# Eight slots of a threshold attention: block transposes and DMA exchanged for TensorE turns with an identity

## The chip, the cores and the metric

The kernel runs on one core of a Trainium2 chip. The metric is the device time of one execution in microseconds, as the median over runs. TensorE (PE) multiplies, with its weight loads shown as PEld; VectorE (DVE), ScalarE (ACT) and GpSimd (POOL) work on vectors; SyncE (SP) issues most DMA transfers. [...]

## The reference

Attention with a threshold, for 8 batches, 8 heads, 576 positions and 64 numbers a head, and then a dense block on the 4608 tokens of 512 numbers:

```
scores = (q @ k^T) / 8
thresh = max(scores) - tau                   # per row
scores = where(scores >= thresh, scores, -1e9)
attn   = exp(scores - max(scores));  attn = attn / (sum(attn) + 1e-9)
x      = attn @ v                            # tokens of 8 heads x 64 = 512
h      = x @ w_in                            # 512 -> 1024
solu   = h * softmax(h)
ln     = (solu - mean) / sqrt(var + 1e-6) * g_ln
out    = ln @ w_out                          # 1024 -> 512
```

All is float32 but the two weight matrices, which arrive as 8-byte floats and are taken apart by integer operations (16 pieces of 512 KB).

## The kernel before

**Slots and rounds.** A slot is one attention step: for a pair of heads (`hp`, four pairs a batch), 128 query rows for each of the two heads, against all 576 keys. There are 144 slots, 18 a batch; two slots (`r` 0 and 1) make a unit, whose product with v is done in one go. The first eight slots are the four units of batch 0, `kind` 0. The program is written out by hand, round by round, under a manual schedule; round `rnd` holds the steps of slot `rnd` and later steps of earlier slots.

**A slot's steps.** `scores` (L480): eight products of 64x64 tiles of the array into two PSUM tiles of 128x576, one a head. `maxes` (L502): VectorE finds the negated row maximum plus tau (`nth`) for each. `ramp` (L517): ScalarE turns scores into distances to the threshold; what lies under the threshold becomes hugely negative. `exps` (L526): the exponential, with the row sum. In the next round `normalise` (L533 to L536): GpSimd adds 1e-9, takes the power -1 and scales both tiles by it. Then `blocks` (L548): VectorE transposes 32x32 blocks of each tile into `T`; after the second slot of a unit three DMAs (L557, L559) move the blocks between partitions into `wT`. Some rounds later (`LAG_PV`, `pv_due`) `attend_steps` (L590) makes the unit's 36 products with v, and `attended` (L622) copies the result into `xh`, one part of the tokens.

**The dense block.** When the four pairs of a group of tokens are there, the group is `ready`: two parts of 128 tokens, each with four steps, at most one a round: two of `ff_h` (L655) and two of `ff_o` (L760), with vector steps between. `ff_o` needs all of w_out (`w2_done`, true from the end of round 16).

**What stands around it in the first rounds.** `whole_pair` (L434) turns q and k of pair 1, 2, 3 of the batch by products with an identity (L345), in rounds 0, 2 and 4; it needs both spare PSUM tiles. These two tiles, p0 and p1, are handed out by `take` from the list `pairs_free`; the products with v and the dense block use them too. The two tiles of `scores` are apart from them and single. One weight piece a round is decoded (L286 to L309 on VectorE, L291 on ScalarE, L319 on GpSimd), until round 15; its raw data are loaded four rounds ahead by SP. `w` has four buffers, `wT` two, `T` two.

Of the kernel before, what the change touches and what calls it, by code (L numbers as in the profile page):

```python
# [8 lines left out]
F32 = mybir.dt.float32  # L9
# [4 lines left out]
ALU = mybir.AluOpType  # L14
# [6 lines left out]
def kernel(  # L21
# [49 lines left out]
    w1 = const.tile([P, NP, DFF], F32, name="w1")  # L71
    w2 = const.tile([P, 2 * NC, DM], F32, name="w2")
    w1_parts = w1.rearrange("p c (a g x) -> p c g a x", g=2, x=32)
    mhalf = const.tile([P, 1], F32, name="mhalf")
    mone = const.tile([P, 2], F32, name="mone")
    mark = const.tile([P, 1], F32, name="mark")
# [143 lines left out]
    def constants():  # L220

        nc.gpsimd.memset(lims[0], 0.0)
        nc.scalar.activation(out=ntau, in_=lims[0], func=AF.Exp)
        make_identity(nc, ident)
        for g in range(2):
            of = 64 + 32 * (1 - g)
            nc.gpsimd.tensor_copy(
                out=swapped[ROWS[1], 32 * g : 32 * g + 32], in_=ident[ROWS[1], of : of + 32]
            )
        nc.gpsimd.memset(mhalf, -0.5)  # L230
        nc.gpsimd.memset(mone, -1.0)
# [282 lines left out]

    def ramp(s, x):
        d = live[s]
        nc.scalar.activation(  # L517
            out=d["w"][x], in_=d["w"][x] if d["loose"] else d["ps"][x][:, 0:S], func=AF.Prelu, bias=d["nth"][x], scale=-1.0,
            alpha=1.0e30,
        )  # L520

    def exps(s):
        d = live[s]
        d["sm"] = sm = small.tile([P, 2], F32, tag="sm", name="sm")
        for x, w in enumerate(d["w"]):
# [279 lines left out]
    pv_due = []  # L805
    for s, (b, kind, hp, r) in enumerate(slots):
        if r == 1:
            pv_due.append((s + LAG_PV + (s < 6 or s in (11, PER - 1, PER + 9)), (b, kind, hp)))

    def first_slot(i):  # L810
        return PER * (i // NP) + 2 * (i % NP)
# [56 lines left out]
    with tc.manual_schedule():  # L868
# [13 lines left out]


        pieces = {r: x for x, r in enumerate(range(16))}
        whole = {0: 1, 2: 2, 4: 3}
        for r, hf, parts in ((0, 0, (0,)), (1, 0, (1, 2)), (3, 1, (0,)), (5, 1, (1, 2))):
            load_at[r] = [lambda hf=hf, parts=parts: load_v(0, hf, parts)]

# [9 lines left out]
        while True:  # L898
# [10 lines left out]
            if rnd == NS:  # L909
# [6 lines left out]
                    cur = None  # L916
                    quarter = 0
                assert quarter != 3
            if rnd == 13:
                prev, cur, quarter = cur, None, 0  # L920
            if (
                cur is None and quarter == 0 and ready and ready[0][0] <= rnd
# [9 lines left out]
            if more:  # L932
                room = SPARE
                if busy and quarter > 1 and preps and rnd + 4 < first_slot(preps[0][3]):
                    room = 0
                while preps and preps[0][0] <= rnd and preps[0][1] <= room:
                    _, n, make, _ = preps.pop(0)
                    items.append(make())
                    room -= n
                scores(rnd, items)  # L940
                if rnd == 0:
                    turned(dict(first, base=576, eased=True), [q_item(0, slice(1, 4))])
                    pairs_free += tags
                idle = quarter == 0 and cur is None and (
                    prev is None or bool(pv_due) and pv_due[0][0] <= rnd
                )
                loose = idle and rnd > NW
                if loose:
                    keeps(rnd, 0)
                    keeps(rnd, 1)  # L950
                maxes(rnd, loose)
                ramp(rnd, 0)
                if rnd == 0:
                    weight_a(0)
                if not loose:
                    keeps(rnd, 0)
                    keeps(rnd, 1)
                ramp(rnd, 1)
                exps(rnd)
            if rnd in whole:  # L960
                whole_pair(whole[rnd])
            if rnd - 1 in live:
                normalise(rnd - 1)
            if rnd - 1 in pieces:
                weight_c(pieces[rnd - 1])
# [22 lines left out]
            if step == ("h", 0):  # L988
                ff_h(cur, 0, rnd + 1 < NS, beside)
                quarter = 1  # L990
            elif step == ("h", 1):
                ff_h(cur, 1, None, beside)
                quarter = 2
                by = rnd + 2 * (rnd == 14)
                late.setdefault(by, []).append(lambda t=cur: (ff_max(t), ff_exp(t)))
                late.setdefault(by + 1, []).append(lambda t=cur: (ff_mul(t), ff_sum(t)))
                middle.setdefault(by + 2, []).append(lambda t=cur: ff_stats(t))
                if rnd + 6 < NS:
                    norms[by + 3] = cur
                else:  # L1000
                    late.setdefault(rnd + 2, []).append(lambda t=cur: ff_norm(t))
                middle.setdefault(by + 3, []).append(lambda t=cur: (ff_norm2(t), ff_swap(t)))

                at = by + 4 if more or not ready or len(ready[0][1][0]) == 1 else rnd + 6
                if cur == (0, 1, 1):
                    middle.setdefault(rnd + 6, []).append(lambda t=cur, at=rnd + 6: ff_turn(t, at))
                else:
                    late.setdefault(at, []).append(lambda t=cur, at=at: ff_turn(t, at))
                if not more:
                    between.append(cur)  # L1010
                    cur = None
                    quarter = 0
            elif step == ("o", 0):
                if prev is not None:
                    ff_o(prev, 0)
                quarter = 3
            elif step == ("o", 1):
                if prev is not None:
                    ff_o(prev, 1)
                    last = not (more or ready or cur or between)  # L1020
                    begin.setdefault(rnd + 1, []).append(lambda t=prev, last=last: ff_out(t, last))
                    late.setdefault(rnd + 1, []).append(lambda t=prev, last=last: ff_store(t, last))
                prev, cur = cur, None
                quarter = 0
            if attending is not None:
# [5 lines left out]
                    ready.append((rnd + 1, [(b // 2,)]))  # L1031
                elif kind < 2 and hp == NP - 1:
                    ready.append((rnd + 1, [(b, kind, 0), (b, kind, 1)]))
            if rnd - 1 in live:
                blocks(rnd - 1)
            for job in late.pop(rnd, []):
                job()
# [55 lines left out]
```

## Time and profile before

| what | value |
|---|---|
| median of 3 runs | 865.01 us (863.66 to 867.64) |
| profiled execution, span from first to last instruction | 867.2 us |
| profiled execution, own time | not listed apart from its span |
| TensorE busy | 822.9 us (95%) |
| VectorE busy | 681.7 us (79%) |
| ScalarE busy | 573.6 us (66%) |
| GpSimd busy | 500.2 us (58%) |
| mean granted TensorE clock | 0.976 |
| DMA | 168.54 MB, mean 194 GB/s |

The span lies inside the range of the three runs, 2.2 us above their median. In the profile, a line such as L502 is a line of the kernel before; `x280` counts instructions; a product in float32 appears as two MATMUL records. Digits of the 40 slices are tenths, 21.7 us a slice. The granted clock is the share of its full clock that TensorE was given.

### The profile page before, as it was taken

The numbers are of one execution on the slowest core, as the hardware profiler recorded it, in microseconds if no ns is written. First come the engines' busy times: TensorE is split into PE (matmuls) and PEld (weight loads), VectorE is DVE, ScalarE is ACT, GpSimd is POOL, SyncE is SP. The second block draws the span as 40 slices with busy tenths as digits, with TensorE's granted clock in tenths as the row PEclk, the third lists the DMA queues.
The fourth block names the chain that finished last, engine by engine and source line by source line (L and its number), as shares of the span: only waits on it lengthen the run. The fifth ranks groups of instructions, "written<-read, shape, count | busy, mean of one in ns | idle before, by whom it ended". The sixth has DMA issues, their size and how long they took to land.

```text
span 867.2 us, 36122 instructions
## 1 busy us (share of the span) xinstructions
PE 822.9 (95%) x15361; PEld 605.8 (70%) x15361; DVE 681.7 (79%) x1248; ACT 573.6 (66%) x1153; POOL 500.2 (58%) x938
## 2 busy tenths in 40 slices
PE   5668799989999999999999999999999999999997
PEld 3446466667677776899777766777777777777655
DVE  4988878878788888888888887888788887787361
ACT  5877876667677767777666766777677776776121
POOL 2886656556756666565656665565666655555120
PEclk9769999999999999999999999999999999999999
DMA  8999887998888878898888787888788787655312
GB/s 256 252 251 227 191 210 181 210 236 210 215 206 226 208 183 214 208 221 203 196 207 225 207 187 185 217 220 207 183 230 229 197 192 180 163 136 139 69 38 62
DMA packets 83712, 168.54 MB, mean 194 GB/s; under 512 B 15448, under 2 KB 45152, under 8 KB 83552
## 3 DMA queue, kind: packets, MB, share of 16 engines
q1 hardware_dynamic: 82416, 164.25, 76.3%
q8 instruction: 120, 1.97, 1.0%
q10 hardware_dynamic: 1136, 2.00, 0.7%
q14 instruction: 40, 0.33, 0.1%
HBM read 46.14 MB, written 9.44 MB: 64 GB/s over the span
## 4 chain that ended last, share of the span: by engine, by line
PE 79%; DMA 8%; DVE 4%; ACT 4%; SPq 2%; issue 2%; POOL 1%; ACTq 0%; DVEq 0%
PE o_ps L760 26%; PE h_ps L655 20%; PE pv L590 14%; PE s_ps L480 14%; DMA wT<-T 6%; PE h_ps L645 3%; ACT w L517 1%; DVE w L502 1%; ACT w L526 1%; DVE T L548 1%; DMA q<-in_q_dram 1%; DMA qT<-flip 1%; SPq L564 1%; DMA k<-in_k_dram 1%; SPq L559 0%
## 5 line engine op out<-in xcount | busy, mean ns | idle before, releaser
L760 PE MATMUL o_ps<-w,uT 64*64 64x256 f32 x4608 | 271.6, 378 | 1.2 <-ACT xe L622 0.6
L502 DVE CUSTOM_DVE_ANT_0 w<-s_ps,tau_t 128x576 f32<-128x576 f32 x280 | 200.0, 751 | 90.0 <-PE s_ps L480 61.6
L517 ACT ACTIVATE w<-s_ps,nth 128x576 f32<-128x576 f32 x280 | 196.9, 739 | 107.0 <-DVE nth L502 89.6
L760 PEld LDWEIGHTS o_ps<-w,uT 64*64 64x64 f32 x4608 | 212.7, 134 | 66.1 <-ACT xh L622 12.1
L536 POOL TENSOR_SCALAR w<-w,sm 128x576 f32<-128x576 f32 x288 | 222.1, 783 | 14.3
L548 DVE STREAM_TRANSPOSE T<-w 128x576 f32<-128x576 f32 x288 | 207.6, 755 | 20.6 <-POOL w L536 19.1
L655 PE MATMUL h_ps<-w,xh 64*64 64x512 f32 x1856 | 221.0, 589 | 0.1
L526 ACT ACTIVATE w<-w,ntau 128x576 f32<-128x576 f32 x288 | 219.7, 767 | 0.0
L590 PEld LDWEIGHTS pv<-wT,v 64*64 64x64 f32 x5760 | 175.2, 138 | 45.4 <-issue 24.5
L480 PE MATMUL s_ps<-kT,qT 64*64 64x64 f32 (+1 forms) x2048 | 177.1, 422 | 13.3 <-ACT w L517 10.9
L590 PE MATMUL pv<-wT,v 64*64 64x128 f32 (+1 forms) x5760 | 178.0, 266 | 10.9 <-DMA wT<-T 7.8
L655 PEld LDWEIGHTS h_ps<-w,xh 64*64 64x64 f32 x1856 | 118.0, 133 | 78.8 <-issue 45.7
L533 POOL TENSOR_SCALAR sm<-sm 128x2 f32<-128x2 f32 x144 | 37.0, 257 | 201.8 <-ACT w L526 198.5
L534 POOL TENSOR_TENSOR sm<-sm,mone 128x2 f32<-128x2 f32 x144 | 108.7, 755 | 12.0
L480 PEld LDWEIGHTS s_ps<-kT,qT 64*64 64x64 f32 x2048 | 73.0, 139 | 21.7 <-ACT w L517 15.7
L622 ACT COPY xh<-pv 128x256 f32<-128x256 f32 x64 | 25.1, 393 | 82.4 <-PE pv L590 82.4
L721 ACT ACTIVATE V<-u,nb,rs 128x1024 f32<-128x1024 f32 x36 | 44.7, 1241 | 39.3 <-POOL nb L711 32.4
L747 DVE STREAM_TRANSPOSE uT<-V 128x1024 f32<-128x1024 f32 x36 | 44.2, 1227 | 18.1 <-DMA V<-u 17.7
L526 ACT ACTIVATION_READ_ACCUMULATOR w<-w,ntau 128x1 f32 x288 | 55.6, 193 | 0.0
L685 DVE TENSOR_TENSOR u<-h_ps,u 128x1024 f32<-128x1024 f32 x36 | 42.8, 1190 | 9.8 <-ACT u L679 9.8
L726 DVE TENSOR_SCALAR u<-u,rs,nb 128x1024 f32<-128x1024 f32 x36 | 35.3, 982 | 17.6 <-ACT V L721 17.6
L670 DVE TENSOR_REDUCE hm<-h_ps 128x1 f32<-128x1024 f32 x36 | 42.9, 1192 | 4.8 <-PE h_ps L645 2.7
(90 smaller groups left out, 568.1 us busy)
## 6 DMA issues: line engine op xcount, KB each, us to landing
wT<-T SPq DMA_DIRECT2D x160, 288.0 KB, 6.7
wT<-T SPq DMA_DIRECT2D x64, 576.0 KB, 5.4
V<-u SPq DMA_DIRECT2D x144, 64.0 KB, 3.3
out_dram<-ob SPq DMA_DIRECT2D x71, 128.0 KB, 2.5
q<-in_q_dram SPq DMA_DIRECT2D x24, 288.0 KB, 5.7
qT<-flip SPq DMA_DIRECT2D x48, 144.0 KB, 4.2
k<-in_k_dram SPq DMA_DIRECT2D x24, 288.0 KB, 6.1
kT<-flip SPq DMA_DIRECT2D x48, 144.0 KB, 3.9
```

The lines of the kernel that those rows point to most:

```text
L480: nc.tensor.matmul(out=ps[h][ROWS[y], ks], lhsT=lhsT, rhs=d["kT"][ROWS[h], ks], start=True, stop=True,)
L502: nc.vector.tensor_tensor_reduce(out=w, in0=ps[:, 0:S], in1=(zero if loose else tau_t).to_broadcast([P, S]), scale=1.0, scalar=BIG, op0=AL ...
L517: nc.scalar.activation(out=d["w"][x], in_=d["w"][x] if d["loose"] else d["ps"][x][:, 0:S], func=AF.Prelu, bias=d["nth"][x], scale=-1.0, al ...
L526: nc.scalar.activation(out=w, in_=w, func=AF.Exp, bias=ntau, scale=1.0, accum_out=sm[:, x : x + 1])
L534: nc.gpsimd.tensor_tensor(out=sm, in0=sm, in1=mone, op=ALU.pow)
L536: nc.gpsimd.tensor_scalar(out=w, in0=w, scalar1=sm[:, x : x + 1], scalar2=1.0, op0=ALU.mult, op1=ALU.mult)
L548: nc.vector.transpose(out=T[:, :, r, h, :], in_=w)
L590: nc.tensor.matmul(out=to, lhsT=d["v"][ROWS[u], (h0 + h - u) % 4 if b > 1 else h0 + h, m ^ 4 * u if m < 8 and b < 2 else m,], rhs=rhs, sta ...
L655: mm = nc.tensor.matmul(out=h[ROWS[y], f], lhsT=x[ROWS[r], c, ROWS[y]], rhs=w1_parts[ROWS[r], c, part ^ r], start=part == 0 and c == 0, st ...
L721: nc.scalar.activation(out=V, in_=u, func=AF.Identity, bias=nb, scale=rs)
L747: nc.vector.transpose(out=uT, in_=d["V"].rearrange("p y (m x) -> p m y x", x=32))
L760: nc.tensor.matmul(out=d["o"][ROWS[z], 512 * (r ^ other) : 512 * (r ^ other) + 256], lhsT=d["uT"][ROWS[r], m].rearrange("p y x -> p (y x)" ...
```

## The change

For the first eight slots (`FRONT = 8`) the path from the distances to the tokens is another one:

- `ramp` writes the distances with their columns in another order, and GpSimd (`clamp`) raises what lies under -10000 to -10000.
- In the next round, `flip` turns each tile by 18 products of 64x64 with an identity into a spare PSUM tile, and `flipped` takes the exponential on the way from PSUM into `wT`. The exponential in place, the normalisation by GpSimd, the block transposes and the block transfers of these slots are left out.
- `front_product` makes a unit's 36 products with v, and 36 more with a tile of ones, which give the row sums. `front_norm` has VectorE add 1e-9, take the reciprocal and multiply, which writes the tokens to `xh` in place of the copy.
- The products of the first three units stand in two consecutive rounds each (3 and 4, 5 and 6, 7 and 8; between the two turns), those of the fourth in round 9. Before, the units' products stood in rounds 5, 7, 9 and 10.
- Pairs 2 and 3 are turned in rounds 1 and 2 instead of 2 and 4.
- The first tokens are ready a round earlier: the first four steps of the dense block stand in rounds 10 to 13 instead of 11 to 14.

```diff
+    ones = const.tile([P, 64], F32, name="ones")
...
+        nc.gpsimd.memset(ones, 1.0)
...
     def ramp(s, x):
         d = live[s]
+        to, of = d["w"][x], d["w"][x] if d["loose"] else d["ps"][x][:, 0:S]
+        if s < FRONT:
+            to = to.rearrange("p (m x c) -> p c m x", c=2, m=NK)
+            of = of.rearrange("p (c m x) -> p c m x", c=2, m=NK)
         nc.scalar.activation(
-            out=d["w"][x], in_=d["w"][x] if d["loose"] else d["ps"][x][:, 0:S], func=AF.Prelu, bias=d["nth"][x], scale=-1.0,
-            alpha=1.0e30,
-        )
+            out=to, in_=of, func=AF.Prelu, bias=d["nth"][x], scale=-1.0, alpha=1.0e30
+        )
+
+    FRONT = 8
+
+    def clamp(s, x):
+        w = live[s]["w"][x]
+        nc.gpsimd.tensor_scalar(
+            out=w, in0=w, scalar1=-1.0e4, scalar2=1.0, op0=ALU.max, op1=ALU.mult
+        )
+
+    def flip(s, h):
+        b, kind, hp, r = slots[s]
+        key = (b, kind, hp)
+        if r == 0 and h == 0:
+            wT = work.tile([P, 2, NK, 2, 2, 32], F32, tag="wT", bufs=2, name="wT")
...
+        w = live[s]["w"][h].rearrange("p (m x) -> p m x", m=NK)
+        tag, t = take("flip")
+        for m in range(NK):
+            for y in range(2):
+                nc.tensor.matmul(
+                    out=t[ROWS[y], 64 * m : 64 * m + 64], lhsT=w[ROWS[y], m],
+                    rhs=swapped[ROWS[1]] if y else ident[ROWS[0], ROWS[0]],
+                    start=True, stop=True,
+                )
+        return tag, t
+
+    def flipped(s, h, tag, t):
+        b, kind, hp, r = slots[s]
+        nc.scalar.activation(
+            out=units[b, kind, hp]["wT"][:, :, h, r],
+            in_=t[:, 0:S].rearrange("p (m x) -> p m x", x=64),
+            func=AF.Exp, bias=ntau, scale=1.0,
+        )
+        pairs_free.append(tag)
+        if h:
+            live.pop(s)
+
+    def front_product(key, ones_too):
...
+        if not ones_too:
+            tag, y = take("pv")
...
+        for m in range(NK):
+            for u in range(2):
+                for h in range(2):
+                    of = P * ones_too
+                    nc.tensor.matmul(
+                        out=y[ROWS[h], u, of : of + P],
+                        lhsT=ones[ROWS[u]] if ones_too
+                        else d["v"][ROWS[u], h0 + h, m ^ 4 * u if m < 8 else m],
+                        rhs=wT[ROWS[u], m, h].rearrange("p r x -> p (r x)"),
+                        start=m == 0, stop=m == NK - 1,
+                    )
+
+    def front_norm(key):
...
+        rec = work.tile([P, 2, P], F32, tag="T", name="rec")
+        nc.vector.tensor_scalar(
+            out=rec, in0=y[:, :, P : 2 * P], scalar1=1e-9, scalar2=None, op0=ALU.add
+        )
+        nc.vector.reciprocal(out=rec, in_=rec)
+        nc.vector.tensor_tensor(
...
+            in0=y[:, :, 0:P].rearrange("p u (r y) -> p u r y", r=2),
+            in1=rec.rearrange("p u (r y) -> p u r y", r=2), op=ALU.mult,
+        )
+        pairs_free.append(tag)
...
         if r == 1:
-            pv_due.append((s + LAG_PV + (s < 6 or s in (11, PER - 1, PER + 9)), (b, kind, hp)))
+            if s >= FRONT:
+                pv_due.append((s + LAG_PV + (s in (11, PER - 1, PER + 9)), (b, kind, hp)))
...
-        whole = {0: 1, 2: 2, 4: 3}
+        whole = {0: 1, 1: 2, 2: 3}
...
-            if rnd == 13:
+            if rnd == 12:
                 prev, cur, quarter = cur, None, 0
...
                 scores(rnd, items)
+                turned_w = [flip(rnd - 1, 0)] if 0 < rnd <= FRONT else []
+                unit = (rnd - 3) // 2
+                if 0 <= unit < FRONT // 2 and unit % 4 != 3:
+                    front_product(slots[2 * unit][0:3], rnd % 2 == 0)
...
                 maxes(rnd, loose)
                 ramp(rnd, 0)
+                if rnd < FRONT:
+                    clamp(rnd, 0)
+                if turned_w:
+                    flipped(rnd - 1, 0, *turned_w.pop())
+                    turned_w = [flip(rnd - 1, 1)]
...
                 ramp(rnd, 1)
-                exps(rnd)
+                if rnd < FRONT:
+                    clamp(rnd, 1)
+                else:
+                    exps(rnd)
+                if turned_w:
+                    flipped(rnd - 1, 1, *turned_w.pop())
+                if 0 <= unit < FRONT // 2:
+                    if unit % 4 == 3 and rnd % 2:
+                        front_product(slots[2 * unit][0:3], 0)
+                        front_product(slots[2 * unit][0:3], 1)
+                    if (rnd % 2 == 0) == (unit % 4 != 3):
+                        key = slots[2 * unit][0:3]
+                        front_norm(key)
+                        if key[2] == NP - 1:
+                            ready.append((rnd + 1, [(*key[0:2], 0), (*key[0:2], 1)]))
             if rnd in whole:
                 whole_pair(whole[rnd])
-            if rnd - 1 in live:
+            if rnd - 1 in live and rnd > FRONT:
                 normalise(rnd - 1)
...
-                by = rnd + 2 * (rnd == 14)
+                by = rnd + 2 * (rnd == 13)
...
-            if rnd - 1 in live:
+            if rnd - 1 in live and rnd > FRONT:
                 blocks(rnd - 1)
```

More of the change, by code (lines that the diff above doesn't have):

```diff
@@ new lines @@
+    FRONT = 8
[9 more added lines that the diff above has]
+            wT = work.tile([P, 2, NK, 2, 2, 32], F32, tag="wT", bufs=2, name="wT")
+            units[key] = dict(
+                wT=wT.rearrange("p a m b c x -> p (a m b c x)").rearrange(
+                    "p (m h r x) -> p m h r x", m=NK, h=2, r=2
+                )
[10 more added lines that the diff above has]
+        return tag, t
@@ new lines, in flipped @@
+    def flipped(s, h, tag, t):
[9 more added lines that the diff above has]
+    def front_product(key, ones_too):
+        b, kind, hp = key
+        unit = units[key]
+        wT = unit["wT"]
+        if not ones_too:
+            tag, y = take("pv")
+            unit["y"] = tag, y.rearrange("p (u n) -> p u n", u=2)
+        y = unit["y"][1]
+        d, h0 = source(b * NP + hp)
+        for m in range(NK):
[9 more added lines that the diff above has]
+                    )
@@ new lines, in front_norm @@
+    def front_norm(key):
+        b, kind, hp = key
+        tag, y = units.pop(key)["y"]
+        if hp == 0:
+            xh[b, kind] = work.tile(
+                [P, NP, 256], F32, tag=f"xh{(2 * b + kind) % 4}", bufs=1, name="xh"
+            )
+        rec = work.tile([P, 2, P], F32, tag="T", name="rec")
+        nc.vector.tensor_scalar(
+            out=rec, in0=y[:, :, P : 2 * P], scalar1=1e-9, scalar2=None, op0=ALU.add
+        )
+        nc.vector.reciprocal(out=rec, in_=rec)
+        nc.vector.tensor_tensor(
+            out=xh[b, kind][:, hp].rearrange("p (r u y) -> p u r y", u=2, r=2),
+            in0=y[:, :, 0:P].rearrange("p u (r y) -> p u r y", r=2),
+            in1=rec.rearrange("p u (r y) -> p u r y", r=2), op=ALU.mult,
+        )
+        pairs_free.append(tag)
```

## The prediction

> **What bounds the kernel now.** I read first the busy times in 40 slices and the table of windows, for where each engine is short; then the chain of waits of the first 200 us, for what ends last there; then the timelines of DVE, PE and POOL round by round. The page:
>
> ```profile
> span 867.2 us, 36122 instructions
> PE 822.9 (95%) x15361; PEld 605.8 (70%) x15361; DVE 681.7 (79%) x1248; ACT 573.6 (66%) x1153; POOL 500.2 (58%) x938
> PE   5668799989999999999999999999999999999997
> PEclk9769999999999999999999999999999999999999
> ```
>
> TensorE is busy 95% of the span, and its idle time lies in the first slices; there its clock is reduced too. By windows (us; busy PE, PEld, DVE, ACT, POOL; then granted clock, DMA share, GB/s):
>
> ```profile
> 20.00:40.00 20.00, 13.84 (x262) 10.13 (x258) 19.53 (x42) 17.82 (x41) 16.91 (x20) 0.67 0.89 237
> 40.00:60.00 20.00, 12.16 (x172) 6.51 (x170) 18.54 (x40) 15.75 (x32) 16.90 (x20) 0.76 1.05 251
> 60.00:80.00 20.00, 17.21 (x241) 12.75 (x240) 14.45 (x31) 12.54 (x25) 12.26 (x16) 0.81 0.95 228
> 200.00:400.00 200.00, 199.77 (x3847) 154.62 (x3843) 168.18 (x306) 140.04 (x278) 123.61 (x240) 1.00 0.84 210
> ```
>
> From 20 to 60 us VectorE is the bound (98% and 93%), TensorE two thirds busy at about 0.7 of its clock. From 200 us on TensorE has no gap, so what the front loses or gains arrives whole at the end. The chain (start, length, what) shows the one long wait of the front:
>
> ```profile
> 53.84 0.74 DVE T L548
> 54.63 0.58 SPq L557
> 55.26 0.60 SPq L559
> 55.92 12.04 DMA wT<-T
> 68.00 3.53 PE pv L590 x65
> ```
>
> The block transfer of the fourth unit (slots 6, 7) takes 12.04 us, and its product waits for it. So the scores of the rounds, from the PE timeline, start at 14.1 (round 1), 18.5, 22.9, 28.4, 33.1, 40.4, 43.2, 48.6, 53.4 (round 9), 62.6, 71.3, 75.7, and 105.6 in round 17. Rounds 1 to 8 follow VectorE: two maxima 1.36 (0.68 from start to start), two transposes 1.36, the weight piece 1.0 + 0.6 + 0.34 + 0.34, together about 5.0 us. Rounds 9 and 10 follow the transfers, 9 us each. VectorE is then the bound again (its maximum of round 11 starts at 72.5, of round 17 at 108.5), and after that TensorE.
>
> By the two instruction streams, the order on TensorE is the same from round 17 to the end. So I forecast when round 17 is reached, and add the difference.
>
> **Part by part.** *Removed* in slots 0 to 7: 16 transposes (16 x 0.68 = 11 us of VectorE, on the path in rounds 1 to 8); 12 block transfers of 4 units with their SP issues (four times 576 KB, on the path in rounds 9 and 10); POOL's add and power (8 x (0.26 + 0.76) us, beside other work); ScalarE's 16 sum reads (about 0.09 us each from start to start) and 4 copies of 0.37, beside. POOL's 16 clamps of 128x576 replace 16 scalings of that form (0.78 each). The ramp's interleaved write I price as before (0.74): the copy into kT that also pairs columns, 0.384 for 128x256, costs no more than the plain xh copy, 0.393.
>
> *Added on TensorE:* per slot two turns of 18 products of 64x64, and per unit 36 products with ones. The identity products of the trace (L345) start every 0.11 us per group of four tiles of the array at full clock (93.24, 93.30, 93.36: two products each 0.055) and every 0.22 at half. A turn uses two tiles instead of four, so 9 x 0.11 = 1.0 us at full clock if the two overlap, 1.9 if not; at half clock double. I take 1.0: tiles ran side by side in every L345 group. The ones cost what a product with v of 72 records does, 1.92 at full clock (3.90 at 36.73, at half).
>
> A round 3 to 8 on TensorE is then scores 0.97 + turns 2.0 + product 1.92 = 4.9 us at full clock, 5.0 with gaps: no less than VectorE's 5.0 before. VectorE has 3.65 left, ScalarE 2 x 0.63 + 2 x 0.67 + 0.62 = 3.2, POOL 2 x 0.74 + 1.28 = 2.8. TensorE becomes the bound of these rounds, and the 11 us taken off VectorE bring nothing by themselves.
>
> *The clock.* In 2 us windows of before the clock steps between 0.5 and 1.0 at about 23.4, 26.8, 33.6, 37.0, 40.4, 43.9, 47.3, 54.1: multiples of 3.4 us, up after a stretch filled by work, down after one with more than about 1 us of idleness (47.3 to 50.7, with 2.7 busy, kept it; 40.5 to 43.9, with 2, lost it). So a filled TensorE runs at 1.0, and each longer stall costs up to 1.7 us more by a half-clock stretch. [...] The trace shows identity products filling 20.2 to 22.4, and the clock rises at 23.4, so they count as work; at half clock a round of 4.9 would take 9.8. [...]
>
> *Rounds 1 and 2.* The pairs' turns (rounds 2 and 4 before) move to rounds 1 and 2, and take both spare PSUM tiles, which each turn of distances now occupies until its exponential. Round 1: scores end at 16.4, the turns of slot 0 at 18.4; the second exponential stands on ScalarE behind the second ramp (its maximum ends at 17.7; two ramps and two exponentials alternate at 0.65 from 17.1), so 19.7; pair turn 1.1; scores of round 2 at 20.9 instead of 18.5. The same chain again (copies of the pair 1.5, maximum, ramp, exponential): round 3 at 26.4 instead of 22.9. TensorE idles some 1.3 us in each, so I add one half-clock stretch, 1.7: 28.1.
>
> *Added on VectorE:* three operations of 128x256 per unit, waiting for the product with ones, with the next weight piece and maximum queued behind. The first and third cost 0.43 and 0.45 by the copy row (L407, 0.425). The reciprocal has no row. Low end: the copy, 0.43. High end: the only division-like rows are POOL's powers, 572 ns for 128x1 and 755 for 128x2 against 234 and 257 for an add; one more element costs 183 against 23, eight times. VectorE's copies of 64 and 256 (0.215, 0.425) give 1.1 ns an element, so 256 x 8 x 1.1 = 2.25 us + 0.15 = 2.4. I take 2.0, since a power is nearer to a division than a copy is. [...]
>
> What waits: from the end of the ones (rounds 4 and 6), VectorE needs 2.9 for the three, 2.3 for weights, 0.75 for the maximum; ScalarE 0.7 + 0.7 for ramp and exponential; only then is the tile free for the second turn: 7.35 us. TensorE has 1.0 + 0.97 + 1.0 + 1.92 = 4.9 to do meanwhile. Stall 2.45 us in rounds 5 and 7, or 0.9 at the copy's price. The longer stall also costs half-clock stretches, 2.5 us for both (of at most 3.4).
>
> *Sum.* Round 9 starts at 28.1 + 6 x 5.0 + 2 x 2.45 + 2.5 = 65.5, against 53.4. Round 9: scores and both products 4.9, the three operations 2.9, transposes and weights 3.6: VectorE's maximum of round 10 at 76.9, of round 11 (another 1.4 + 1.4 + 2.3) at 82.0, against 72.5. From there to the maximum of round 17 VectorE needed 36.0, of which some 3 us idle; the same work, with the first dense tile a round earlier, I take at 35.0. Round 17's maximum: 117.0 against 108.5, +8.5. Gained are the 12 us transfer and its neighbour; paid are 3.5 + 1.7 in rounds 1 and 2, 7.4 in 5 and 7, and the wait for the last norm. Profiled span 867.2 + 8.5 = 875.7; it lies 2.2 above the median of the runs, so 873.5, rounded to 873.
>
> **Rivals.** *Cheap reciprocal* (0.43): round 9 at 28.1 + 30 + 1.8 = 59.9, round 10's maximum at 69.7, round 17's at 109.8: +1.3, 866. For it: every other VectorE row here runs at about one element a nanosecond. Chance 0.22.
>
> *TensorE fills from round 1 on* (faster). If in addition the pair turns find their tiles free when the PE queue reaches them, each round is TensorE's 4.9 and round 9 starts at 14.1 + 8 x 4.9 = 53.3, 6.6 before the last case: -5.3, 860; any slack I priced too high (the weights' 1.06 rows, seen beside a busy POOL, shrink to 0.65) makes it 857. It decides where the stall of round 5 stays under about 0.3 us and rounds 1 and 2 under 5. For: VectorE is the proven bound of 20 to 60 us, and a third of TensorE lay idle. Against: single spare tiles chain the three engines. Chance 0.20.
>
> *The two tiles do not overlap:* a turn takes 1.9; 16 more turn-microseconds, of which the stalls absorb some 7: +17, 882. Against: the L345 rows. Chance 0.13. [...] Chance 0.03. That the transfers stay is excluded: the SP stream lacks their 12 issues.
>
> **Numbers.** The forecast has 0.42. Half a per cent, 4.3 us, is about what a measurement of this kernel can tell from no change: 860.7 to 869.3. Slower: 0.42 + 0.13 + 0.03 = 0.58; same 0.22; faster 0.20. The forecast's own range is 869 to 880 (reciprocal 1.3 to 2.4, no or all half-clock stretches); holding 8 in 10 it must reach into both sides: 858 to 886.
>
> **What would show it.** Right: reciprocal near 2 us; TensorE idle before the second turn in rounds 5 and 7 with the exponential as releaser; scores of round 9 near 65 and of round 17 near 114; a turn about 1.0 us at full clock; clock mostly 1.0 from 28 to 65. Wrong: reciprocal under 0.6 us; round 9 before 58; the span after round 17 differing from before by more than 2 us, which would mean that the front is not the whole story.

## The result, and the profile after

The changed kernel takes 892.31 us (median of 4 runs, 891.75 to 893.84), the kernel before beside it 864.65 (863.66 to 867.64): ratio 1.031, 95% interval 1.028 to 1.035. Forecast were 873 us and a range of 858 to 886, so it is slower, as forecast, but by 27.7 us in place of 8. The profiled execution has a span of 890.9 us.

The page of the changed kernel:

```profile
span 890.9 us, 37824 instructions
PE 836.1 (94%) x16225; PEld 625.7 (70%) x16225; DVE 681.3 (76%) x1244; ACT 572.8 (64%) x1133; POOL 514.4 (58%) x923
PE   5677769999999999999999999999999999999997
PEclk9998989999999999999999999999999999999999
```

TensorE's weak slices are 0 to 5 (before: 0 to 4), but its clock there is near full now: the idle time isn't filled, it is only clocked higher. The windows (busy PE, PEld, DVE, ACT, POOL; granted clock, DMA share, GB/s; the clock of before was 0.67, 0.76 and 0.81 in them) say the same:

```profile
20.00:40.00 20.00, 14.70 (x475) 11.70 (x474) 7.32 (x18) 10.31 (x22) 14.50 (x8) 1.00 0.33 85
40.00:60.00 20.00, 13.45 (x368) 11.05 (x358) 12.01 (x26) 8.71 (x13) 11.91 (x7) 0.91 0.49 139
60.00:80.00 20.00, 13.46 (x356) 11.40 (x360) 13.05 (x21) 9.02 (x15) 12.89 (x7) 0.89 0.17 55
```

From 20 to 80 us no engine is full: TensorE 69% busy, VectorE 54%, ScalarE 47%, GpSimd 66%. The bound is then a chain through several engines. Where the time went is read from the starts of the first maximum of a round (VectorE's timeline; L502 before, L504 after):

| | round 1 | 3 | 5 | 7 | 9 | 10 | 11 | 17 | span, from round 17 |
|---|---|---|---|---|---|---|---|---|---|
| before | 16.2 | 26.8 | 36.7 | 46.6 | 56.5 | 64.6 | 72.5 | 108.5 | 758.7 |
| after | 14.8 | 32.4 | 49.3 | 66.9 | 82.3 | 92.3 | 96.8 | 134.1 | 756.8 |
| forecast | | | | | | 76.9 | 82.0 | 117.0 | 758.7 |

Rounds 1 to 9 take 67.5 us in place of 40.2, 27.3 more, and the loss arises there alone: round 1 starts 1.4 us earlier than before, rounds 9 to 17 take as long as before (51.8 and 52.0), and the stretch from round 17 on is 1.9 shorter. So the two profiled executions differ by 23.7 us over the whole span (890.9 and 867.2). The chain of waits of the changed kernel from one maximum to the next (start, length, what; VectorE's two maxima follow each other at 32.43 and 33.11):

```profile
32.52 0.67 DVE w L504
...
33.29 0.79 ACT w L523
...
34.22 2.14 POOL w L531
...
36.43 2.13 POOL w L531
...
38.65 1.28 POOL w L321
...
40.29 0.42 DVE em L294
40.71 0.67 DVE w L504
```

Maximum, ramp, both clamps on GpSimd, the product of the last weight piece (L321) behind them, the split of the next weight piece on VectorE, which needs the exponent buffer that this product reads, and behind the split the next maximum: a closed loop of 8.2 us. VectorE's waits between 14 and 90 us name it (engine, line, what it waited for; us, times, longest):

```profile
DVE em L288 <- POOL w L321: 26.6, 7, 6.0
```

In the kernel before, the split did not wait for this product: in round 5 (GpSimd, then VectorE) the product has ended at 39.63 when the split's turn comes.

```profile
38.35 1.28 POOL L319 TENSOR_TENSOR w<-w,em 128x512 f32<-128x512 f32 x1
40.70 0.42 DVE L286 TENSOR_SCALAR em<-raw 128x512 int32<-128x512 int32 x1
```

The length of the loop comes from the clamp. The line's answer (ns min/median/max, first and last start):

```profile
L531 POOL TENSOR_SCALAR w<-w x16: 2131/2133/2931, 12.5 to 71.0; 128x576 f32<-128x576 f32 x16
```

A maximum with a bound takes GpSimd 2.13 us, where the scaling of the same shape took 0.74 to 0.78 before:

```profile
L536 POOL TENSOR_SCALAR w<-w,sm x288: 740/751/1343, 16.9 to 799.8; 128x576 f32<-128x576 f32 x144
```

### The profile page after: what moved, and what is told of

Its sections match the earlier page's. It is cut to its first block, busy times and chain, and to the rows that moved or that the text cites. A ratio compares the mean times of both kernels' runs of the same rounds, so it can differ in the third digit from the quotient of the medians.

```text
span 890.9 us, 37824 instructions
## 1 busy us (share of the span) xinstructions
PE 836.1 (94%) x16225; PEld 625.7 (70%) x16225; DVE 681.3 (76%) x1244; ACT 572.8 (64%) x1133; POOL 514.4 (58%) x923
## 4 chain that ended last, share of the span: by engine, by line
PE 77%; DMA 6%; POOL 6%; DVE 3%; ACT 3%; issue 2%; SPq 2%; ACTq 0%; POOLq 0%; DVEq 0%
PE o_ps L845 26%; PE h_ps L740 20%; PE s_ps L482 14%; PE pv L675 13%; POOL w L531 4%; PE h_ps L730 3%; DMA wT<-T 3%; ACT w L523 1%; DMA raw<-in_moe_w_out_dram 1%; DVE w L504 1%; POOL w L321 1%; DMA v<-in_v_dram 1%; ACT w L611 1%; SPq L822 1%; DMA k<-in_k_dram 0%
## 5 line engine op out<-in xcount | busy, mean ns | idle before, releaser
L504 DVE CUSTOM_DVE_ANT_0 w<-s_ps,tau_t 128x576 f32<-128x576 f32 x280 | 200.1, 751 | 88.4 <-PE s_ps L482 54.4
L845 PEld LDWEIGHTS o_ps<-w,uT 64*64 64x64 f32 x4608 | 214.1, 133 | 63.1 <-ACT xh L707 12.1
L621 POOL TENSOR_SCALAR w<-w,sm 128x576 f32<-128x576 f32 x272 | 210.4, 785 | 13.6
L633 DVE STREAM_TRANSPOSE T<-w 128x576 f32<-128x576 f32 x272 | 195.8, 754 | 18.7 <-POOL w L621 17.2
L611 ACT ACTIVATE w<-w,ntau 128x576 f32<-128x576 f32 x272 | 207.3, 766 | 0.0
L675 PEld LDWEIGHTS pv<-wT,v 64*64 64x64 f32 x5472 | 161.6, 135 | 36.8 <-issue 14.2
L482 PE MATMUL s_ps<-kT,qT 64*64 64x64 f32 (+1 forms) x2048 | 172.7, 416 | 6.6 <-ACT w L523 5.6
L675 PE MATMUL pv<-wT,v 64*64 64x128 f32 (+1 forms) x5472 | 162.4, 260 | 8.7 <-DMA wT<-T 6.4
L618 POOL TENSOR_SCALAR sm<-sm 128x2 f32<-128x2 f32 x136 | 33.6, 247 | 187.9 <-ACT w L611 184.7
L619 POOL TENSOR_TENSOR sm<-sm,mone 128x2 f32<-128x2 f32 x136 | 100.9, 742 | 11.3
L611 ACT ACTIVATION_READ_ACCUMULATOR w<-w,ntau 128x1 f32 x272 | 52.2, 192 | 0.0
L531 POOL TENSOR_SCALAR w<-w 128x576 f32<-128x576 f32 x16 | 36.4, 2278 | 23.8 <-ACT w L523 15.4
L811 DVE TENSOR_SCALAR u<-u,rs,nb 128x1024 f32<-128x1024 f32 x36 | 35.0, 973 | 17.5 <-ACT V L806 17.5
```

Source lines behind the costliest of these rows:

```text
L482: nc.tensor.matmul(out=ps[h][ROWS[y], ks], lhsT=lhsT, rhs=d["kT"][ROWS[h], ks], start=True, stop=True,)
L504: nc.vector.tensor_tensor_reduce(out=w, in0=ps[:, 0:S], in1=(zero if loose else tau_t).to_broadcast([P, S]), scale=1.0, scalar=BIG, op0=AL ...
L531: nc.gpsimd.tensor_scalar(out=w, in0=w, scalar1=-1.0e4, scalar2=1.0, op0=ALU.max, op1=ALU.mult)
L611: nc.scalar.activation(out=w, in_=w, func=AF.Exp, bias=ntau, scale=1.0, accum_out=sm[:, x : x + 1])
L619: nc.gpsimd.tensor_tensor(out=sm, in0=sm, in1=mone, op=ALU.pow)
L621: nc.gpsimd.tensor_scalar(out=w, in0=w, scalar1=sm[:, x : x + 1], scalar2=1.0, op0=ALU.mult, op1=ALU.mult)
```

## The experiments

The theory at the start (A): the clamp's price, through the loop above, makes the loss. Its rival (B): the rounds are long for another reason, and a shorter clamp only uncovers it. Both turned out to be half of it.

Times of a group of runs stand beside its own runs of the kernel before, on the same chip. "Round 9" is the start of that round's first maximum in the profiled execution.

### The clamp and the loop behind it

*e1_scale: the clamp becomes a scaling.*

```diff
-            out=w, in0=w, scalar1=-1.0e4, scalar2=1.0, op0=ALU.max, op1=ALU.mult
+            out=w, in0=w, scalar1=1.0, scalar2=1.0, op0=ALU.mult, op1=ALU.mult
```

> GpSimd's clamp (maximum, then product with 1) becomes two products with 1: same tile, same place in GpSimd's queue, same waits, but without the lower bound of -10000. Theory A (the clamp costs 2.13 us instead of the 0.74 of a scaling, and each round waits for two of them and the weight piece behind them): the form costs 0.74 to 0.78; a round then is maximum 0.85, ramp 0.75, exponential 0.7, ramp 0.75, clamp 0.75, weight product 1.3, weight split 0.75, together about 5.9 us instead of 8.4; round 9's maximum at about 63 instead of 82.3 and the time 870 to 875. Theory B (the turns through one spare tile and the products with ones are the price, GpSimd only fills the wait): rounds stay at 8 us or more and the time at 886 or more.

*e2_noclamp: both calls of the clamp are taken out.*

> The clamp is left out (no lower bound of the distances); GpSimd keeps only the weight products in rounds 1 to 8, and the turns wait for the ramp itself. Theory A: the loop over GpSimd is gone, rounds of 5.0 to 5.6 us as TensorE, VectorE and the late reciprocal allow, round 9's maximum at 57 to 62, time 865 to 872, some 3 to 6 us under the run with two products. Theory B: 884 or more.

*e3_weight_first: the clamp stays, and the weight piece's product (weight_c) is recorded ahead of the round's clamps.*

```diff
+                if rnd - 1 in pieces and rnd <= FRONT:
+                    weight_c(pieces[rnd - 1])
...
-            if rnd - 1 in pieces:
+            if rnd - 1 in pieces and rnd > FRONT:
                 weight_c(pieces[rnd - 1])
```

> The clamp stays as it is at 2.13 us; only the weight piece's product on GpSimd is written ahead of the round's two clamps (rounds 1 to 8), so that the next weight split on VectorE, and with it the next maximum, no longer stands behind the clamps. Theory A with the loop as said (clamps, then weight product, then weight split, then the next maximum): GpSimd's own work of 2 x 2.2 + 1.3 = 5.7 us sets the round instead of 8.4; round 9's maximum at about 64 and the time 870 to 876. If the clamp's length alone counts and not its place ahead of the weight piece: no more than 3 us gained, 888 or more. Theory B: 888 or more too.

*e4_product_first: the clamp multiplies first and takes the maximum second.*

> The same clamp with its two operations in the other order: product with 1 first, then the maximum. If any maximum on GpSimd is slow, the form stays at about 2.1 us and the time at 892; if only the order with the maximum first is slow, it costs about 0.75 and the run comes out like the one with two products, 870 to 875.

| run | median us | ratio to before | round 1 | round 9 |
|---|---|---|---|---|
| e1_scale | 878.0 | 1.013 (1.009 to 1.017) | 16.0 | 70.6 |
| e2_noclamp | 879.4 | 1.015 (1.010 to 1.020) | 15.9 | 74.4 |
| e3_weight_first | 881.6 | 1.017 (1.012 to 1.022) | 16.7 | 73.6 |
| e4_product_first | 893.1 (one run) | | 15.8 | 82.7 |

The clamp's line, in e1_scale and then in e4_product_first:

```profile
L531 POOL TENSOR_SCALAR w<-w x16: 670/672/1212, 12.8 to 61.1; 128x576 f32<-128x576 f32 x16
```

```profile
L531 POOL TENSOR_SCALAR w<-w x16: 2131/2138/2947, 12.6 to 71.6; 128x576 f32<-128x576 f32 x16
```

The maximum is what costs, at either place of the pair (e4 is a single run; its clamp's row and its rounds are those of the changed kernel). With a scaling the time falls by 14 us (892.3 to 878.0; by the ratios, 1.031 to 1.013, some 16), and rounds 1 to 9 by 12.9. With the slow clamp kept but taken out of the loop (e3) it falls by 10.7 us. So the clamp's price, through this loop, is the cause of about half of the loss. What missed: taking the clamp away altogether gains nothing over the cheap one, and rounds 1 to 9 stay at 6.8 us each with the cheap clamp and 7.3 without it. In e2 VectorE waits no more for GpSimd's product between 14 and 90 us, but for the scores of TensorE, so another path sets the rounds there:

```profile
DVE w L504 <- PE s_ps L482: 7.4, 5, 2.0
```

### What isn't the other half

These four stand on e1_scale.

*e5_no_reciprocal: the reciprocal becomes a product with one.*

> As e1_scale (clamps as products), and the reciprocal is replaced by a product with 1 of the same tile, so the first four units are not divided by their sums. Theory A (VectorE is the bound of the rounds that hold a norm): a reciprocal of 1.75 us becomes 0.35 to 0.45, the rounds from 4, 6 and 8 shrink from 6.8 to about 5.5 and round 9 by 1.3; together 4 to 5 us, 872 to 874 against e1_scale's 878. If the norm is hidden behind the turns: within 1.5 us of e1_scale.

*e6_pairs_back: the pair turns are put back, `whole = {0: 1, 2: 2, 4: 3}`.*

> As e1_scale, and pairs 2 and 3 are turned in rounds 2 and 4 again, as in the kernel before. Theory A (in rounds 1 and 2 the pair turns wait for both spare tiles, which the turns of distances hold until their exponentials; round 2 to 4 take 8.1 and 8.6 us in e1_scale): round 1 and round 3 lose their pair turn, 2 to 4 us gained, 874 to 876. Rival: in round 4 the pair turn must wait for the first unit's norm, since that holds a spare tile, and gives back as much: 878 or more.

*e7_short_ones: the ones product has 4 of its 36 matmuls.*

> As e1_scale, and only the first 4 of the 36 products with ones of each unit are made (the sums then cover a ninth of the columns), 1.7 us less of TensorE in rounds 4, 6, 8 and 9. If TensorE is the bound of these rounds: 4 x 1.7, about 6 us less, 872. If VectorE is (theory A): its norm starts no earlier than its maximum's end, 0.8 us a round earlier at most, 875 to 877.

*e8_last_unit: the turned path for slots 6 and 7 alone, no clamp, with the unit's turned tile in one of the buffers of T; slots 0 to 5 take the block transfers as before.*

> The turned path for slots 6 and 7 alone (no clamp; pairs turned in rounds 0, 2 and 4); slots 0 to 5 go as in the kernel before, and the first dense tile is still a round earlier. It takes away the block transfer that ended last before (12 us, rounds 9 and 10 of 9 us each) and pays for it with four turns, one product with ones and one reciprocal. If those two rounds are worth their 18 - 12 = 6 us: round 10's maximum at 60 to 62 instead of 64.6 and 859 to 863. If rounds 10 to 17 take their 42 to 44 us anyway and the unit before's transfer now ends last: 863 to 867, no difference.

| run | median us | ratio to before | round 9 | round 17 |
|---|---|---|---|---|
| e1_scale | 878.0 | 1.013 (1.009 to 1.017) | 70.6 | 123.1 |
| e5_no_reciprocal | 878.6 | 1.015 (1.010 to 1.019) | 69.7 | 121.2 |
| e6_pairs_back | 881.9 | 1.018 (1.013 to 1.023) | 69.3 | 121.8 |
| e7_short_ones | 878.2 | 1.015 (1.011 to 1.019) | 71.0 | 123.2 |
| e8_last_unit | 870.6 | 1.007 (1.004 to 1.010) | 60.2 | 112.2 |

None of the three suspects alone moves round 9 by more than 1.3 us. e8 shows the least loss: it keeps before's pace until round 8 (52.8 against 51.8) and loses in rounds 8 to 10, 17.5 us against 12.8. In its chain the unit's two products (60.1 to 64.5) and its division (64.5 to 67.1) stand one behind the other there, and the next maximum (70.3) behind both; the turned unit's own work took longer than the wait for the 12 us transfer that it replaced. These runs also show how loosely the end follows the front: from round 17 to the end the spans of all kernels here lie between 752 and 760 us, so a gain of under some 4 us in the front can't be read from the time.

### The order on ScalarE, and a shorter weight product

*e9_exp_first: e1_scale, with the exponential of the round before ahead of the round's own ramp.*

```diff
+                if turned_w:
+                    flipped(rnd - 1, 0, *turned_w.pop())
+                    turned_w = [flip(rnd - 1, 1)]
                 ramp(rnd, 0)
                 if rnd < FRONT:
                     clamp(rnd, 0)
-                if turned_w:
-                    flipped(rnd - 1, 0, *turned_w.pop())
-                    turned_w = [flip(rnd - 1, 1)]
```

> The kernel after, with the clamp as a scaling (no lower bound, as in the run that scales), and in rounds 1 to 8 the exponential of the round before, row 0, put ahead of the round's own first ramp on ScalarE. In the run that scales alone the maxima start at 16.0 (round 1) and 70.6 (round 9), 6.8 us a round, 878.0 us. Theory C (a loop through ScalarE and the spare tile: maximum, ramp 0.8, exponential 0.7, second turn 1.2 and then the scores of the next round on TensorE): the exponential no longer waits for the maximum, the second turn starts 1.5 to 2 us earlier, rounds of 5.2 to 5.9, round 9 at 58 to 63, time 867 to 872. Theory D (VectorE's queue: two maxima 1.4, the weight's four steps 0.7, 0.7, 0.4 and 1.4, half of a division 1.3 = 5.9 a round, and more where SyncE or GpSimd delay a step): round 9 at 68 to 71, time 876 to 879.

*e10_exp_first_no_reciprocal: e9 with e5's edit.*

> As the run with the exponential first, and the four reciprocals are products with one (the first four units are left undivided): 1.75 to about 0.4 each, 1.35 us in every other round on VectorE. Alone, this took nothing off the run that scales. Theory C: after the exponential is moved TensorE is next at 5.0 to 5.2 us a round, the reciprocal is in VectorE's idle time, and round 9 comes within 1 us of the run with the exponential first. Theory D, or both loops of nearly equal length: round 9 comes 3 to 5 us earlier than in that run (4 reciprocals, 1.35 us each).

*e11_exp_first_no_clamp: e9 with e2's and e3's edits.*

> The exponential first, no clamp at all on GpSimd, and the weight piece's product on GpSimd put at the head of the round: the whole turned path with nothing on GpSimd but the weight's product. Theory C: round 9 at 56 to 61, time 864 to 870, near the kernel before (865). Theory D: round 9 at 66 to 70, time 874 to 878, since VectorE's work a round is the same.

*e12_short_piece: in weight_c,*

```diff
-        nc.gpsimd.tensor_tensor(out=dst, in0=dst, in1=e.bitcast(F32), op=ALU.mult)
+        n = 32 if x < 8 else 512
+        nc.gpsimd.tensor_tensor(
+            out=dst[:, 0:n], in0=dst[:, 0:n], in1=e.bitcast(F32)[:, 0:n], op=ALU.mult
+        )
```

> As the run with the exponential first, and GpSimd's weight product takes 32 of 512 columns in the first eight pieces (the rest of these columns stays unscaled): 1.25 us becomes about 0.2, and VectorE's last weight step, 1.43 us beside that product and 0.34 alone, should come back to 0.34. Theory D: VectorE has 1 us less in every round, round 9 comes 6 to 8 us earlier than in the run with the exponential first, if that one still stands at 68 or more. Theory C: rounds are TensorE's by then; round 9 moves by 0 to 2 us.

| run | median us | ratio to before | round 3 | round 9 |
|---|---|---|---|---|
| e9 | 880.5 | 1.020 (1.018 to 1.023) | 29.1 | 70.3 |
| e10 | 877.9 | 1.019 (1.015 to 1.022) | 29.3 | 67.9 |
| e11 | 876.0 | 1.016 (1.013 to 1.020) | 29.5 | 69.1 |
| e12 | 878.7 | 1.017 (1.014 to 1.021) | 28.8 | 68.9 |

Theory C falls: round 9 stays where it was (70.3), where C needed 58 to 63. One thing blurs this: between 30 and 68 us TensorE stands still for 4.7 us in e9, against 1.8 in e1_scale, with nothing in the profile that it waited for, and this may hide a part of a gain. Theory D is right on the pace of e9 and e11, if not on the time of e9 (880.5 for 876 to 879); its 3 to 5 us for e10 came as 2.5, and its 6 to 8 us for e12 as 1.4, since round 8 lost again what rounds 4 to 7 had gained (round 8 at 59.9 against 63.1). VectorE's groups from 36 to 56 us in e11 and in e12, the last step of the weight's split:

```profile
L294 DVE TENSOR_SCALAR em<-raw 128x512 int32<-128x512 int32 x3 | 4.5, 1503 | 0.0
```

```profile
L294 DVE TENSOR_SCALAR em<-raw 128x512 int32<-128x512 int32 x4 | 1.7, 421 | 0.0
```

GpSimd's product holds this step up. In e11 it takes 1.50 us, with the short product 0.42.

### The last waits moved

*e13_gain_early: e9 with `if rnd == 1: gains()` for `rnd == 3`. e14_division_late: also front_norm of the first three units after weight_b and weight_a. e15: also the short product. e16: e14 without the clamp.*

> The run with the exponential first (clamp as a scaling), with the gain turn in round 1, where two spare tiles are free, not in round 3. Theory E (VectorE stands 4.6 us at the gain turn's result because the one spare tile is busy): round 3 shrinks from 8.1 to about 5, maxima from round 4 on come 2.5 to 3.5 us earlier than in the run with the exponential first (round 4 at 34, round 9 at 67), time 877 to 878. Rival (the wait covers something else that is late): round 4 at 36 to 37, nothing gained by round 9.

> As the run with the gain turn early, and in rounds 4, 6 and 8 the division stands behind the weight's split on VectorE, not ahead of it. Theory E (order of VectorE's queue: the weight's 2.4 to 3.9 us wait for a division that waits for the ones product): the even rounds shrink from 6.7 and 9.0 to 5.0 to 6.5, round 9 another 3 to 5 us earlier (62 to 64), time 872 to 874. Rival (VectorE's and TensorE's work itself, 5.9 us a round with GpSimd beside it): round 9 less than 1.5 us earlier.

> As the run with the division late, and GpSimd's weight product takes 32 of 512 columns in the first eight pieces (the rest of those columns stays unscaled). Theory E: what is left is TensorE's 5.0 to 5.2 a round; round 9 at 57 to 60. Rival: round 9 at 64 or later.

> The whole computation: exponential first, gain turn early, division late, no clamp on GpSimd. Theory E: round 9 at 59 to 62, time 867 to 871, still not under the kernel before (865), since VectorE's work a round (maxima 1.4, weight 2.4 to 3.5, half a division 1.3) is no less than before's, where the block turns were 1.4. Rival: round 9 at 66 or later, time 873 or more.

| run | median us | ratio to before | round 1 | round 3 | round 9 |
|---|---|---|---|---|---|
| e13 | 882.1 | 1.019 (1.015 to 1.023) | 16.3 | 32.4 | 72.7 |
| e14 | 882.0 | 1.020 (1.014 to 1.027) | 15.6 | 31.7 | 73.3 |
| e15 | 879.4 | 1.016 (1.012 to 1.020) | 16.1 | 31.8 | 68.1 |
| e16 | 878.5 | 1.016 (1.012 to 1.021) | 16.2 | 32.3 | 67.6 |

Theory E falls too. VectorE's wait for the gain turn moved with it and grew, from 4.7 us in e9 to 6.0 in e13 (waits of 14 to 90 us, e13):

```profile
DVE gs L251 <- PE g_ps L250: 6.0, 1, 6.0
```

And the late division (e14) made TensorE wait for it, since it gives the tile of the products back later:

```profile
PE pv L580 <- DVE xh L600: 4.2, 2, 2.9
```

In e16, with these waits moved and no clamp, rounds 3 to 9 still take 35.4 us, 5.9 each. Its window of 32 to 68 us:

```profile
32.00:68.00 36.00, 32.96 (x996) 27.56 (x996) 33.07 (x58) 24.05 (x41) 8.23 (x8) 1.00 0.44 134
```

TensorE is busy for 32.96 of 36 us and VectorE for 33.07. Of TensorE's 3.0 idle us, 2.0 are of the kind that shows no releaser ("issue"), most of them in one pause inside the product with ones of round 4:

```profile
PE pv L580 <- issue: 1.6, 1, 1.6
```

What it waited for there stays open; the kernel before has no such pause between 30 and 68 us. Two more runs on e16 lengthen one engine each:

*e17_turns_twice: `for m in [*range(NK)] * 2` in flip. e18_reciprocal_three_times: two more `nc.vector.reciprocal(out=rec, in_=rec)`.*

> The whole computation with the exponential first, gain turn early, division late and no clamp (878.5 us, maxima 16.2 in round 1, 32.3 in round 3, 67.6 in round 9), with every identity product of the turns made twice: 72 in place of 36, 1.05 us more a turn, 2.1 a round. TensorE sets the rounds: round 9 comes 6 x 2.1 = 12.6 us after round 3 later than now (round 3 to 9: 48 in place of 35.4), and rounds 1 to 3 grow by 4. VectorE sets them: round 3 to 9 grows by less than 5.

> The same kernel with the reciprocal taken three times in a row (which gives the same value): 3.5 us more on VectorE in rounds 4, 6, 8 and 9. VectorE sets the rounds: round 3 to 9 grows by about 10 us (45 in place of 35.4). TensorE sets them and VectorE has its idle time: grows by under 4.

e17 takes 893.6 us (1.034, 1.026 to 1.042), its rounds 3 to 9 take 44.6 us: 9.2 more, of the 12.6 added. e18 takes 889.9 (1.029, 1.023 to 1.035), rounds 3 to 9 take 47.3: 11.9 more, for 10.5 added. What is added to VectorE arrives in full, as the second expectation had it for a bound VectorE; TensorE, by the first, lies between the two limits and had about 3.4 us of slack in six rounds. So both engines are on the path, and each waits for the other when it is the shorter. VectorE in e17, then TensorE in e18, waits between 24 and 66 us:

```profile
DVE w L504 <- PE s_ps L482: 12.2, 4, 5.5
```

```profile
PE pv L580 <- DVE xh L602: 6.4, 2, 3.2
```

That VectorE is full isn't shown by this. The products wait for the tile that the division gives back, so a longer division lengthens that chain whether VectorE has time left or not; and in e15, where GpSimd's product is short, VectorE is busy for 27.75 of the same 36 us, and rounds 3 to 9 take 36.2 all the same:

```profile
32.00:68.00 36.00, 32.81 (x976) 27.33 (x980) 27.75 (x57) 23.38 (x39) 9.43 (x18) 1.00 0.43 131
```

TensorE's own work allows less than 5.9: in e16 it goes from the scores of round 8 to those of round 9 in 5.1 us without a wait.

```profile
60.62 1.16 PE L482 MATMUL s_ps<-kT,qT 64*64 64x64 f32 x14
65.74 1.15 PE L482 MATMUL s_ps<-kT,qT 64*64 64x64 f32 x14
```

Whether all these rounds could come near that and the 5.0 of before isn't shown; no run joins the short product of e15 with the missing clamp of e16. No version here beats the kernel before.

## Why the prediction was wrong, step by step

**The clamp was priced as a scaling, and this is the step that failed.** "POOL's 16 clamps of 128x576 replace 16 scalings of that form (0.78 each)", and GpSimd's 2.8 us a round were put beside other work. No row of before showed a maximum on GpSimd, so the price had no upper end, and none was given. It measured 2.13: GpSimd has 5.5 us of work a round, and the maximum of the next round stands behind it.

**The loop wasn't seen.** GpSimd's queue was summed, not followed. The weight piece's product stands behind the clamps in it, VectorE's next split needs that product's buffer, and the maximum stands behind the split. Before, the same product stood behind the scalings (38.35 to 39.63 in round 5), and VectorE's two transposes stood between; now the transposes are gone, and the split comes to wait. This and the clamp: 14 of the 27.7 us of loss, and 14 of the 19 us between the forecast of 873 and the 892.3 measured (e1_scale). With the clamp as cheap as I had it, the kernel takes 878, inside the range, 5 over the forecast. A part of that nearness is luck: the maximum of round 17 starts at 123.1 in e1_scale, 6.1 after the forecast, and the rest of its span is 5.4 shorter than the 758.7 that I put there.

**"VectorE has 3.65 left" left the division out of the round.** Before round 9, the division was charged as a stall of TensorE in rounds 5 and 7 alone. It measures 0.46 + 1.78 + 0.34 from start to start, 1.3 a round, nearly the 1.36 that the removed transposes took. With two maxima of 0.68 and a split of 3.0 (1.9 without GpSimd's hold), VectorE's round in e16 is 5.7 us, not less than before. From round 3 to round 9 e16 loses 5.7 us against the kernel before (35.4 against 29.7). The forecast's total for this stretch was near all the same: from scores to scores 37.4, with 4.9 for the two stalls and 2.5 for half-clock stretches; e1_scale takes 39.5 (28.7 to 68.2). But its parts were others. The stall before the second turn, with the exponential as releaser, is there in the changed kernel (3.6 us in round 5, 3.3 in round 7), inside the clamp's loop, and in rounds 4, 6 and 8 too (1.7 to 2.7); with the cheap clamp it is 1.5 in round 5 and nothing in round 7, where I had 2.45 in each.

**The half-clock stretches** (1.7 in rounds 1 and 2, 2.5 later) cost nothing in e1_scale: the granted clock stood at 1.00 from 14 to 80 us, also from 20 to 32, where TensorE was idle for a third of the time:

```profile
20.00:32.00 12.00, 8.14 (x283) 6.17 (x278) 5.63 (x14) 8.13 (x20) 3.83 (x4) 1.00 0.57 149
```

So the rule that I read from the kernel before, that a stretch of 3.4 us with more than about 1 us of idleness loses the clock, doesn't hold as I put it. In the changed kernel, with longer stalls (up to 3.6 us there, 1.6 in e1_scale), the clock was 0.91 from 40 to 60 us.

**Rounds 1 and 2** were forecast to put round 3 back by 3.5 to 5.2. In the changed kernel rounds 1 to 3 take 17.6 us against 10.6, 7 more. With the cheap clamp they take 13.8 (e1_scale), 3.3 more than before and about the lower forecast; in e16, where the gain turn stands in round 1 too, 16.1. That the pair turns and the turns of distances pass one after the other through the spare tiles is what e13's chain suggests (turn, exponential, both ramps, exponential, pair turn, copies, scores from 16.4 to 23.7); no run isolates it.

**Right were** the prices of the pieces that had rows, and the reciprocal. From VectorE's timeline, a division of the changed kernel:

```profile
41.98 0.42 DVE L596 TENSOR_SCALAR rec<-pv 128x256 f32<-128x256 f32 x1
42.44 1.75 DVE L599 RECIPROCAL rec<-rec 128x256 f32<-128x256 f32 x1
44.22 0.42 DVE L600 TENSOR_TENSOR xh<-pv,rec 128x256 f32<-128x256 f32 x1
```

Forecast 0.43, 2.0 and 0.45. A full turn was priced at 1.0 us with its two tiles beside each other; e9's chain has turns of 0.97 to 1.17 at full clock. The ones product was priced at 1.92 and took 1.97 there:

```profile
36.34 0.97 PE flip L549 x33
37.39 1.97 PE pv L580 x70
```

The 0.03 in the sum of chances was for a clock that identity products lower, which no run shows: it stood at 1.00 from 20 to 40 us of the changed kernel, with TensorE 73% busy, and 320 of the 475 records there are such products.

**Rounds 9 to 17** went nearly as forecast. In round 9 the two products and the division follow each other:

```profile
82.31 4.14 PE pv L580 x110
86.47 0.44 DVE rec L596
86.93 1.76 DVE rec L599
89.06 1.43 DVE T L633 x2
```

From the maximum of round 11 to that of round 17 the forecast had 35.0 and 37.3 were measured. From round 17 on the difference to before was -1.9 us, within the 2 that I allowed; over all kernels it was -6.7 to +1.6, so that bound was too narrow as a rule. The rival of a cheap reciprocal was wrong by its price (0.43 against 1.75), and taking the reciprocal away brought nothing in e5 and 2.5 us at round 9 in e10. Of the other rivals, the two tiles do overlap (a turn takes 0.97 to 1.17 us, where 1.9 was forecast without overlap), and TensorE doesn't fill from round 1 on (69% busy from 20 to 80 us).

## What to carry to other kernels

An engine that is "beside" is safe only when its queue has been followed as well as summed: ask which buffers the instructions behind the new one hold, and whose next step needs them. An operation without a row of its kind on that engine needs a high end to its price, even where its shape is well known. And when work is moved off the bound engine, count what comes back to it for the same data: here a division of 1.3 us a round for transposes of 1.36.

## What the hardware showed

GpSimd's time for one shape differed with the operation: 128x576 fp32 took 0.67 us as two products (e1_scale), and 2.13 as a maximum and a product in either order (the changed kernel, e4_product_first), 3.2 times as long.

An operation of VectorE took longer beside a product of GpSimd. In e16, between 32 and 68 us, VectorE's L294 starts 0.17 to 0.18 us after the start of GpSimd's product and ends 0.27 to 0.29 us after its end, five times. Two of them (start, length; VectorE's timeline, then GpSimd's):

```profile
48.85 1.50 DVE L294 TENSOR_SCALAR em<-raw 128x512 int32<-128x512 int32 x1
53.42 1.51 DVE L294 TENSOR_SCALAR em<-raw 128x512 int32<-128x512 int32 x1
```

```profile
48.68 1.40 POOL L321 TENSOR_TENSOR w<-w,em 128x512 f32<-128x512 f32 x1 [6.31 <-DVE em L311]
53.24 1.40 POOL L321 TENSOR_TENSOR w<-w,em 128x512 f32<-128x512 f32 x1 [3.17 <-DVE em L311]
```

Where no product runs beside it, in round 8, the same operation takes 0.42 us, and with the short product it takes 0.42 as well (e12). So I read the 1.1 us between 0.42 and 1.50 as a wait for the product's end that is counted as busy; what makes it wait isn't shown. By that, an estimated 5.4 of VectorE's 33.07 busy us in e16 (five rounds of 1.1) are waiting for GpSimd.
